# Attention in units of 64 queries: stacked heads in the four quarters of TensorE

## The chip, the cores and the metric

The kernel runs on one core of a Trainium2 chip. The metric is device time in microseconds (us). The core's engines are TensorE (PE, with its weight loads listed as PEld), VectorE (DVE), ScalarE (ACT), GpSimd (POOL) and SyncE (SP), which here issues all DMAs. Each engine runs its own instructions in the order in which the program emitted them; semaphores order the engines among each other.

## What is computed

Causal attention (2 batches, 12 heads, 448 tokens, head width 64, f32) feeds two feed-forward layers. The change lies in the attention alone.

```python
scores = q @ k.T / 8                      # per head, 448 x 448
scores = where(upper triangle, -1e9, scores)
attn = exp(scores - rowmax);  attn /= rowsum + 1e-9
x = attn @ v                              # to (896 tokens, 768)
h = x @ w_in;  x = (h * sigmoid(h)) @ w_out          # 768 -> 2048 -> 768
h = x @ w_in2; solu = h * softmax(h); ln = layernorm(solu) * g; out = ln @ w_out2
```

## The kernel before

Two heads make a pair: their 64-wide q and k lie one above the other in the 128 partitions (head 0 in rows 0 to 63, head 1 in 64 to 127). There are 12 pairs; pairs 0 to 5 are batch 0. `ORDER` is a table of steps written out by hand, in which each step is a letter for the work, the pair, and what part of it; a step emits its instructions at once, so the table sets the order on every engine. The letters:

- `q`, `v`, `w`: a DMA of a pair's q and k, of its v, of a weight chunk.
- `So`, `Sa`, `Sb`, `Sc`: score products on PE into one of four PSUM slots of two banks (`/2` is the slot). For each head, query tiles c = 0, 1, 2 of 128 queries are multiplied with 128, 256 and 384 keys (`scores`, L174). The two heads use the two row halves of the PE array, each with all 128 output columns, and run side by side. The last 64 queries of both heads stand stacked in one tile with 448 keys (`scores_last`, L184). Its two row halves write the same banks, so it is made in two passes, held apart by a relay on SP (`f`, L193).
- `m` (L204, DVE): scale, mask and row maximum of one unit, PSUM to SBUF. `e` (L210, ACT): exp with row sum, in place. `r` (L216, L217, DVE): reciprocals. `n` (L224 on POOL, L222 on ACT, L226 on DVE): multiplication by them; a closing `G`, `A` or `V` names the engine.
- A pair has seven units of 128 rows: three query tiles for each of two heads, 128, 256 and 384 wide, and the stacked one, 448 wide: 2 x (128 + 256 + 384) + 448 = 1984 columns.
- `T` (L238, PE): transposes of a pair's 64 x 128 blocks, in two halves of 16. `x` (L255 on ACT, L253 on DVE): their eviction, in four pieces of 768, 256, 512 and 512 columns.
- `P` (L264, PE): attn times v. The two heads use the two column halves of the array; per head four products of 448, 320, 192 and 64 columns. `h` and `l`: the result split into a rounded part and a rest.
- `ca`, `sh`, `sl`, `rh`, `sp`, `wl`: preparation of the first weight chunks from their 64-bit form (`ca` is L291 on ACT, `wl` is L358 on POOL). `g`: a quarter of the first feed-forward product (L427 to L429, 9 instructions) for two blocks of batch 0, which depend on pairs 0 to 5 alone.

After the table the feed-forward products run on PE; at L427 with output tile h the first of them for batch 1 begins. From there on, weights are prepared by `feed`, one chunk after the other, behind the products. A pair's buffers rotate: four for q and k, four for the exponentials, four PSUM slots.

Of the kernel before, what the change touches and what calls it, by code (L numbers as in the profile page):

```python
# [8 lines left out]
F32 = mybir.dt.float32  # L9
# [9 lines left out]
C = 64  # L19
# [32 lines left out]
UNITS = [(0, 2), (1, 2), (0, 0), (1, 0), (0, 1), (1, 1), (0, 3)]  # L52

# [7 lines left out]
So0/1 Sa0/2 m0.00 m0.10 e0.00 Sb0/0 m0.02 m0.12 e0.02 f0 v5 Sc0 e0.12 v3 e0.10 m0.03 q4 v6 m0.01 Sa1/3 e0.03 m0.11  # L61
e0.01 Sb1/1 m1.10 e0.11 Sb2/2 m1.00 f1 m1.12 v0 Sc1 e1.00 f2 r0 w0 e1.10 m1.02 Sa2/0 n0.10G e1.12 m1.03 n0.12G e1.02
Sc2 m1.11 n0.03G m1.01 e1.03 m2.10 Sa3/3 m2.00 e1.11 m2.12 n0.00G n0.11G e1.01 m2.03 Sb3/1 e2.00 n0.02G m2.02 f3 Sc3
e2.10 m2.11 e2.03 n0.01G r1 Sb4/0 m3.02 e2.11 n1.11G f4 m2.01 q5 e2.12 n1.03G m3.10 v1 T0.0/2 m3.12 e2.02 v7 m3.00
n1.02G m3.11 w1 e2.01 T0.1/3 m3.03 v2 x0.0A Sc4 n1.12G m3.01 v9 r2 x0.1A n1.01G Sa4/1 x0.2V ca0 e3.03 n2.01G x0.3V
T1.1/2 q8 n1.00G e3.10 m4.00 w2 P0/3 m4.10 n2.03G e3.01 m4.01 w3 m4.11 e3.00 m4.03 n2.00G q6 e3.02 n1.10G m4.02
e3.12 n2.11G T1.0/0 m4.12 h0A n2.02G x1.3V Sa5/1 e3.11 n2.12G l0 x1.1A x1.0A x1.2V T2.1/3 n2.10G e4.02 r3 T2.0/0
m5.00 n3.10G e4.11 sh0 P1/2 n3.00G x2.1A x2.3V x2.0A n3.11G m5.12 n3.02G e4.12 x2.2V P2/0 e4.03 m5.10 n3.12G m5.02
h1A sl0 n3.01G e4.10 l1 e4.00 Sb5/3 e4.01 h2V n3.03G T3.0/1 e5.12 f5 q7 r4 T3.1/2 sh1 n4.12G ca3 l2 Sc5 e5.00 x3.2V
x3.0A n4.02G Sa6/0 x3.3V q9 x3.1A n4.11G e5.10 m5.11 Sb6/1 ca1 m6.00 n4.01G m6.12 P3/2 f6 e5.02 v4 n4.03G m5.03  # L70
e5.11 m5.01 e5.03 n4.10G m6.10 m6.02 n4.00G e5.01 T4.1/3 rh0 h3A T4.0/0 sh2 r5 x4.3A Sc6 l3 n5.01G x4.2A sl1 x4.0A
n5.00G Sa7/2 q10 m6.01 x4.1A m6.03 n5.10G e6.12 P4/3 n5.11G m7.00 m6.11 e6.00 n5.12G m7.12 e6.02 m7.02 n5.02G e6.01
m7.10 Sb7/0 h4V e6.10 n5.03G T5.0/1 e7.02 f7 v10 l4 Sc7 e6.11 x5.0V e7.12 T5.1/2 x5.1V e6.03 Sb8/3 rh1 Sa8/1 x5.3A
f8 w4 r6 m7.01 x5.2A n6.02G Sc8 m7.03 e7.00 e7.10 m7.11 n6.01G P5/2 m8.01 e7.01 n6.12G m8.10 sp1 m8.03 e7.11 n6.11G
m8.12 e7.03 m8.02 n6.10G Sa9/0 n6.00G m8.11 h5A n6.03G m8.00 sp0 l5 T6.0/3 e8.01 r7 Sb9/1 e8.12 x6.1V T6.1/2 n7.11G
f9 x6.0V v11 e8.10 Sc9 n7.01G w5 x6.3A m9.02 n7.02G v8 x6.2A P6/3 m9.10 q11 e8.11 m9.11 n7.03G m9.01 n7.00A e8.00
m9.00 n7.12V n7.10G e8.02 m9.03 T7.1/2 wl1 e8.03 m9.12 T7.0/1 x7.2A r8 Sa10/0 x7.3A x7.0V n8.00G n8.10G h6A Sb10/2
n8.01G e9.12 x7.1V m10.00 f10 n8.12G P7/1 l6 e9.10 e9.03 m10.12 n8.11G m10.10 e9.02 n8.02V n8.03G m10.02 e9.00
T8.0/3 h7V e9.01 T8.1/0 wl0 x8.1A l7 e9.11 Sc10 sh3 x8.0A r9 Sa11/1 x8.3V n9.01G n9.02A x8.2V ca2 n9.00G P8/3 n9.11G
n9.10A m10.01 e10.00 m10.03 n9.03G e10.10 e10.12 m11.00 m10.11 n9.12V e11.00 Sb11/0 m11.02 h8A T9.1/2 f11 m11.10  # L80
e10.11 Sc11 m11.12 e10.02 l8 T9.0/1 e10.01 sl2 e10.03 g0 x9.2V e11.02 r10 m11.01 n10.10G e11.12 x9.3V n10.03G x9.1A
g1 m11.11 e11.01 n10.01V n10.00G x9.0A n10.02V n10.11G m11.03 n10.12A e11.11 T10.0/2 rh2 e11.03 sl3 T10.1/1 w6 rh3
e11.10 P9/0 x10.2A x10.0V w7 x10.3A r11 sh4 n11.02A n11.00G n11.12V h9A n11.10G x10.1V P10/1 ca4 n11.01V n11.03A
n11.11V l9 sp2 T11.1/2 sp3 wl2 T11.0/0 ca5 x11.3V g2 x11.0V wl3 x11.2V sh5 x11.1V P11/2 sl4 h10V rh4 l10 g3 w8 h11A
l11
# [4 lines left out]
def fused(ctx, tc, qk, vv, w1, w2, w3, w4, gl, out):  # L90
# [13 lines left out]
    gain = const.tile([128, KF2], F32, name="gain")  # L104

# [16 lines left out]
    with tc.manual_schedule():  # L122
# [4 lines left out]
        mask3 = att.tile([128, S], F32, name="mask3", bufs=1)  # L127
# [4 lines left out]
        QC = 3  # L132
        KEYS = [(0, 0), (0, 1), (0, 2), (1, 0), (1, 1), (1, 2), (0, 3)]
        COL = {u: n for n, u in enumerate(UNITS)}
        AT = {(0, 0): 0, (0, 1): 1, (0, 2): 3, (1, 0): 6, (1, 1): 7, (1, 2): 9, (0, 3): 12}
        wide = lambda c: min(128 * (c + 1), S)

        st = [att.tile([128, 44], F32, name=f"st{n}", tag=f"st{n}", bufs=1) for n in range(4)]
# [37 lines left out]
        def scores_last(p, n, first):  # L176
            k, q = raws[p]
            if first:
                sb[p] = slot(n)
            dst = scs[p, 0, 3] = sb[p][:, :, 256:256 + S // 2]  # L180
            made = []
            for j in range(2):
                r, z = slice(64 * j, 64 * j + 64), j if first else 1 - j
                made.append(nc.tensor.matmul(dst[:, z], q[QC][r], k[r, S // 2 * z:S // 2 * (z + 1)],  # L184
                                             start=first, stop=not first))
            if first:
                passes[p] = made
            else:
                for m in made:
                    behind(m, relays[p])  # L190

        def relay(p):
            relays[p] = nc.sync.nop(nofuse=True)  # L193
            for m in passes[p]:
                behind(relays[p], m)

        def ep(p, u):
            return es[p % EB][:, AT[u]:AT[u] + 4].rearrange("q b k -> q (b k)")[:, :wide(u[1])]

        def maxes(p, u):  # L200
            o, m = ep(p, u), (mask3 if u[1] == 3 else mask)[:, S - wide(u[1]):]
# [975 lines left out]
```

## Time and profile before

| | |
|---|---|
| Runs | 401.73, 400.26, 401.11 us; median 401.11 |
| Profiled execution | 401.01 us; its span, first to last instruction, is 399.2 us |
| Granted TensorE clock, mean over the span | 1.00 |
| PE busy in the span | 98% |
| DVE, ACT, POOL busy | 74%, 70%, 46% |
| DMA | 50.04 MB, mean 125 GB/s |

Busy shares are averages over stages that differ. The attention takes roughly the first fifth of the span, and matmuls are pipelined with modelled ends, so PE's share alone does not say how near it is to its limit. Instructions on ACT and DVE overlap too: the distance between two starts is what one of them costs its engine.

### The profile page before, as it was taken

The page shows a single profiled execution, that of the slowest core. Times are in us where ns is not written, and L with a number is a line of the kernel's source. Part 1 is how long each engine was busy: PE and PEld are TensorE (multiplying, and loading weights), DVE is VectorE, ACT ScalarE, POOL GpSimd, SP SyncE. Part 2 cuts the span into 40 slices and gives each one's busy share as a digit, 9 for nine tenths or more (in the row PEclk, how much of TensorE's full clock was granted, in tenths as well). Part 3 has the DMA queues.
Part 4 walks back from the last instruction along what each step waited for, and adds up shares of the span by engine and source line. Part 5 has one row for each costly group of instructions (what it writes and reads, how often), then busy time and mean ns, then how long its engine had stood idle before and what let it go on. Part 6 is the DMA issues. An engine that isn't in the chain of part 4 may idle for free.

```text
span 399.2 us, 7580 instructions
## 1 busy us (share of the span) xinstructions
PE 392.2 (98%) x2622; PEld 363.1 (91%) x2622; DVE 295.9 (74%) x693; ACT 281.1 (70%) x653; POOL 183.9 (46%) x219
## 2 busy tenths in 40 slices
PE   7999999999999999999999999999999999999996
PEld 5777678899999999999999999999988888999996
DVE  4999999677675765768566667776899997666943
ACT  5999999655665473766577777785757875898630
POOL 2998783223554372556665445554001000496450
PEclk9999999999999999999999999999999999999999
DMA  7775322134434333437344567777023320011121
GB/s 246 248 276 173 121 91 65 56 92 151 150 98 125 112 113 112 120 120 201 115 150 129 164 178 233 244 252 217 18 81 98 101 79 0 2 61 39 42 79 61
DMA packets 19766, 50.04 MB, mean 125 GB/s; under 512 B 2320, under 2 KB 4496, under 8 KB 19728
## 3 DMA queue, kind: packets, MB, share of 16 engines
q1 hardware_dynamic: 19728, 49.56, 39.4%
q8 instruction: 21, 0.34, 0.4%
q14 instruction: 17, 0.14, 0.1%
HBM read 46.80 MB, written 2.75 MB: 124 GB/s over the span
## 4 chain that ended last, share of the span: by engine, by line
PE 89%; DVE 8%; ACT 2%; issue 1%; DVEq 0%; ACTq 0%; SPq 0%
PE h L427 8%; PE h L429 8%; PE h L428 8%; PE x L264 5%; PE ps L942 5%; PE h L598 4%; PE h L597 4%; PE h L599 4%; PE ps L944 4%; PE ps L943 4%; PE h L865 3%; PE h L867 3%; PE h L866 3%; PE x L174 3%; PE x L238 3%; DVE e L204 3%
## 5 line engine op out<-in xcount | busy, mean ns | idle before, releaser
L291 ACT ACTIVATE wr<-wr 128x384 f32<-128x384 f32 x96 | 56.9, 592 | 9.4 <-DMA wr<-w_in 9.4
L428 PE MATMUL h<-l,wh 128*128 128x448 f32 x174 | 61.3, 352 | 0.0
L427 PE MATMUL h<-h,wh 128*128 128x448 f32 x174 | 61.3, 352 | 0.0
L429 PE MATMUL h<-h,wl 128*128 128x448 f32 x174 | 61.3, 352 | 0.0
L224 POOL TENSOR_TENSOR e<-e,st 128x128 f32<-128x128 f32 (+3 forms) x70 | 44.0, 666 | 20.1 <-DVE st L217 15.1
L321 DVE SCALAR_TENSOR_TENSOR pw<-wr,pw 128x384 uint32<-128x384 uint32 x77 | 43.0, 559 | 12.9 <-ACT pw L317 12.7
L446 POOL TENSOR_TENSOR gl<-sg,gh 128x448 fp32r<-128x448 f32 x29 | 32.8, 1152 | 38.9 <-ACT sg L444 38.9
L210 ACT ACTIVATE e<-e,st 128x128 f32<-128x128 f32 (+3 forms) x84 | 43.8, 536 | 4.2 <-DVE st L204 4.2
L358 DVE TENSOR_TENSOR wl<-pw,wh 128x384 fp32r<-128x384 f32 x29 | 16.2, 557 | 31.7 <-ACT wh L354 31.7
L354 ACT ACTIVATE wh<-pw 128x384 fp32r<-128x384 f32 x29 | 14.3, 494 | 35.2 <-PE h L428 27.4
L204 DVE CUSTOM_DVE_ANT_0 e<-x,mask 128x128 f32<-128x128 f32 (+3 forms) x84 | 32.9, 445 | 5.2 <-PE x L174 5.1
L428 PEld LDWEIGHTS h<-l,wh 128*128 128x128 f32 x174 | 32.9, 189 | 0.1
L427 PEld LDWEIGHTS h<-h,wh 128*128 128x128 f32 x174 | 32.9, 189 | 0.0
L429 PEld LDWEIGHTS h<-h,wl 128*128 128x128 f32 x174 | 32.9, 189 | 0.0
L896 POOL TENSOR_TENSOR s<-s,mhalf 128x1 f32<-128x1 f32 x7 | 4.2, 596 | 62.3 <-DVE s L895 62.3
L865 PE MATMUL h<-w3h,h 128*128 128x512 f32 x84 | 32.0, 381 | 0.6 <-ACT h L893 0.6
L866 PE MATMUL h<-w3l,h 128*128 128x512 f32 x84 | 31.9, 379 | 0.0
L867 PE MATMUL h<-w3h,l 128*128 128x512 f32 x84 | 31.8, 379 | 0.0
L597 PE MATMUL h<-gh,wh 128*128 128x448 f32 x90 | 31.7, 352 | 0.0
L599 PE MATMUL h<-gh,wl 128*128 128x448 f32 x90 | 31.7, 352 | 0.0
L598 PE MATMUL h<-gl,wh 128*128 128x448 f32 x90 | 31.7, 352 | 0.0
L358 POOL TENSOR_TENSOR wl<-wx,wh 128x384 fp32r<-128x384 f32 x21 | 21.2, 1011 | 22.7 <-ACT wh L354 22.7
(299 smaller groups left out, 1115.1 us busy)
## 6 DMA issues: line engine op xcount, KB each, us to landing
wr<-w_in SPq DMA_DIRECT2D x96, 384.0 KB, 3.2
qk<-qk_in SPq DMA_DIRECT2D x11, 480.0 KB, 4.6
v<-vv_in SPq DMA_DIRECT2D x12, 256.0 KB, 5.2
out<-o SPq DMA_DIRECT2D x14, 192.0 KB, 1.9
qk<-qk_in SPq DMA_DIRECT2D x2, 128.0 KB, 2.3
qk<-qk_in SPq DMA_DIRECT2D x1, 224.0 KB, 2.6
gain<-gl_in SPq DMA_DIRECT2D x1, 4.0 KB, 3.8
```

The costliest lines, as they stand in the source:

```text
L204: nc.vector.tensor_tensor_reduce(o, scs[p, u[0], u[1]], m, -SCALE, 3.0e38, ALU.add, ALU.min, st[p % 4][:, COL[u]:COL[u] + 1])
L210: nc.scalar.activation(ep(p, u), ep(p, u), AF.Exp, bias=st[p % 4][:, n:n + 1], scale=-1.0, accum_out=st[p % 4][:, 8 + n:9 + n])
L224: eng.tensor_tensor(ep(p, u), ep(p, u), r.to_broadcast([128, wide(u[1])]), ALU.mult)
L291: nc.scalar.activation(high, high, AF.Copy, scale=DOWN)
L427: nc.tensor.matmul(ps[:, :S], wh, rh, start=turn == 0 and k % NB == 0, stop=False)
L428: nc.tensor.matmul(ps[:, :S], wh, rl, start=False, stop=False)
L429: nc.tensor.matmul(ps[:, :S], wl, rh, start=False, stop=turn == 1 and k % NB == NB - 1)
L597: nc.tensor.matmul(ps[:, :S], wh, rh, start=f == CF[0], stop=False)
L598: nc.tensor.matmul(ps[:, :S], wh, rl, start=False, stop=False)
L599: nc.tensor.matmul(ps[:, :S], wl, rh, start=False, stop=f == CF[-1])
L865: nc.tensor.matmul(ps[:, n], yh[k][:, at], wh, start=k == 0, stop=False)
L866: nc.tensor.matmul(ps[:, n], yh[k][:, at], wl, start=False, stop=False)
```

## The change

The unit of attention becomes 64 queries of both heads of a pair, stacked: unit u holds queries 64u to 64u + 63 of head 0 and head 1 in its two row halves, and has 64(u + 1) keys. A pair has seven units, 64 to 448 wide: 1792 columns. Every score product now has 64 rows of weights and 64 output columns, a quarter of the PE array. In units 1 to 4 (`SWAPPED`) head 0 goes to the lower half of the output partitions and head 1 to the upper; so a unit in 0, 5, 6 uses the two quarters on one diagonal of the array and a unit in 1 to 4 the two on the other. The lists `STEPS_A` and `STEPS_B` cut the products so that, from pair 1 on, groups of four equally long ones in the four quarters follow each other (320, 128, 64 columns; 256 and 128). Both products of a unit write one PSUM bank, in different partitions. Pair 0 has an order of its own (`Sx`, `Sy`, `Sz`) that follows its three DMA pieces.

Transposes stay 32 per pair, their evictions become 896, 128, 640 and 384 columns. `P` has the same columns, but cut at the units where the head order turns (`RUNS`): eight products per head in place of four. The relay and the second mask go. A pair's q and k are 448 KB, before 480. In the table, five weight conversions (`ca`) go from ACT to POOL, a sixth goes behind the table, and one weight chunk less is prepared in it (`EARLY` was fed one further). The letters for engines are dealt anew: normalizations 74 on POOL, 3 on ACT, 7 on DVE (before 70, 6, 8); evictions 26 on ACT and 22 on DVE (before 24 and 24); `h` 9 on ACT and 3 on DVE (before 8 and 4).

```diff
-UNITS = [(0, 2), (1, 2), (0, 0), (1, 0), (0, 1), (1, 1), (0, 3)]
+UNITS = S // C
+SWAPPED = (1, 2, 3, 4)
+BANKS = ((6, 0), (4, 2), (5,), (3, 1))
+RUNS = ((0, 1, 0), (1, 5, 1), (5, 7, 0))
 ORDER = """
-So0/1 Sa0/2 m0.00 m0.10 e0.00 Sb0/0 m0.02 m0.12 e0.02 f0 v5 Sc0 e0.12 v3 e0.10 m0.03 q4 v6 m0.01 Sa1/3 e0.03 m0.11
+q1 v0 q2 v1 Sx0/0 q3 m0.1 Sy0 m0.0 v2 e0.1 e0.0 Sz0 m0.2 m0.3 e0.2 m0.4 e0.3 m0.5 e0.4 q4 m0.6 Sa1/2 e0.5 w0 v3 e0.6
...
-        def scores(p, c):
-            k, q = raws[p]
-            for j in range(2):
-                r = slice(64 * j, 64 * j + 64)
-                t = sb[p][:, 1 - j] if c == 1 else sa[p][:, j, 384:] if c == 0 else sa[p][:, j]
-                scs[p, j, c] = dst = t[:, :wide(c)]
-                nc.tensor.matmul(dst, q[c][r], k[r, :wide(c)], start=True, stop=True)
...
+        def scores(p, steps):
+            a = raws[p]
+            for u, lo, hi in steps:
+                n = next(n for n, bank in enumerate(BANKS) if u in bank)
+                t = (sa, sb)[n // 2][p][:, n % 2]
+                o = sum(wide(v) for v in BANKS[n][:BANKS[n].index(u)])
+                scs[p, u] = t = t[:, o:o + wide(u)]
+                for j in range(2):
+                    r, z = slice(64 * j, 64 * j + 64), 64 * (j ^ (u in SWAPPED))
+                    nc.tensor.matmul(t[z:z + 64, lo:hi], a[r, 0, C * u:C * u + C], a[r, 1, lo:hi], start=True, stop=True)
...
+        STEPS_A = [(6, 0, 320), (4, 0, 320), (6, 320, 448), (2, 0, 128), (0, 0, 64), (2, 128, 192)]
+        STEPS_B = [(5, 0, 256), (3, 0, 256), (5, 256, 384), (1, 0, 128)]
...
+        PARTS_T = [[(0, range(UNITS)), (3, range(6, UNITS))], [(1, range(2, UNITS)), (2, range(4, UNITS))]]
+        HALVES = [[(u, kb) for kb, us in part for u in us] for part in PARTS_T]
...
             for z in range(NKB):
-                for j in range(2):
-                    nc.tensor.matmul(t[64 * j:64 * j + 64, 128 * z:S], v[:, j, z], aT[p][:, z, j, 128 * z:],
-                                     start=z == 0, stop=z == NKB - 1)
+                for lo, hi, swap in RUNS:
+                    sl = slice(C * max(lo, 2 * z), C * hi)
+                    for h in range(2):
+                        j = h ^ swap
+                        if sl.start < sl.stop:
+                            nc.tensor.matmul(t[64 * j:64 * j + 64, sl], v[:, j, z], aT[p][:, z, h, sl],
+                                             start=z == lo == 0, stop=z == NKB - 1, skip_group_check=True)
...
-        def conv_a(n, c):
+        def conv_a(n, c, eng=None):
             r = wraw[n, c]
             high = r[:, :, 1].bitcast(F32)
-            nc.scalar.activation(high, high, AF.Copy, scale=DOWN)
+            if eng is nc.gpsimd:
+                eng.tensor_tensor(high, high, down.to_broadcast([128, CH]), ALU.mult)
+            else:
+                nc.scalar.activation(high, high, AF.Copy, scale=DOWN)
...
-        fed[0] = EARLY + 1
-        pend.append(EARLY)
+        fed[0] = EARLY
```

On PE, around the middle of the attention, the order before reads as follows (L184 and L174 are score products, L238 transposes, L264 attn times v; the columns after the tile names are outputs x moving columns, and the count).

```order
L264 MATMUL x_586<-aT,v_168 64x64 x2
L238 MATMUL x_609<-ident,e_97 128x64 x16
L238 MATMUL x_628<-ident,e_97 128x64 x16
L184 MATMUL x_579<-qk 128x224 x2
L174 MATMUL x_579<-qk 128x256 x2
L174 MATMUL x_661<-qk 128x384 x2
L174 MATMUL x_661<-qk 128x128 x2
L264 MATMUL x_673<-aT,v_597 64x448 x2
L264 MATMUL x_673<-aT,v_597 64x320 x2
L264 MATMUL x_673<-aT,v_597 64x192 x2
L264 MATMUL x_673<-aT,v_597 64x64 x2
```

Transposes and scores follow each other there without a change of form. The same round of the changed kernel (L160 are score products, L204 transposes, L231 attn times v):

```order
L231 MATMUL x_354<-aT,v_146 64x64 x2
L204 MATMUL x_390<-ident,e_98 128x64 x16
L204 MATMUL x_411<-ident,e_98 128x64 x16
L160 MATMUL x_432<-qk 64x320 x4
L160 MATMUL x_432<-qk 64x128 x4
L160 MATMUL x_432<-qk 64x64 x4
L160 MATMUL x_450<-qk 64x256 x4
L160 MATMUL x_450<-qk 64x128 x4
L231 MATMUL x_463<-aT,v_150 64x64 x2
L231 MATMUL x_463<-aT,v_150 64x256 x2
L231 MATMUL x_463<-aT,v_150 64x128 x2
L231 MATMUL x_463<-aT,v_150 64x192 x2
```

Before, scores and transposes share one tile form, 64 rows by 128 columns, and PE changes form twice a round; now scores are 64 by 64, and it changes three times. From the first warm-up product to the first product of batch 1 the whole order has 24 changes of form before and 37 now.

On POOL, pairs 2 and 3 before (L224 are normalizations, e_99 and e_100 the exponentials of the two pairs):

```order
L224 TENSOR_TENSOR e_99<-e_99,st_103 128x256
L224 TENSOR_TENSOR e_99<-e_99,st_103 128x384 x2
L224 TENSOR_TENSOR e_99<-e_99,st_103 128x128
L224 TENSOR_TENSOR e_100<-e_100,st_104 128x128 x2
L224 TENSOR_TENSOR e_100<-e_100,st_104 128x256
```

There POOL does nothing but normalizations. Now (L190 are normalizations, L259 the weight conversion that stood on ACT):

```order
L190 TENSOR_TENSOR e_99<-e_99,st_103 128x384
L190 TENSOR_TENSOR e_99<-e_99,st_103 128x256
L259 TENSOR_TENSOR wr<-wr,down 128x384
L190 TENSOR_TENSOR e_100<-e_100,st_104 128x128
L190 TENSOR_TENSOR e_100<-e_100,st_104 128x192
L190 TENSOR_TENSOR e_100<-e_100,st_104 128x384
```

The conversion now stands in POOL's queue ahead of pair 3's normalizations; three more stand ahead of those of pairs 4 and 5, the fifth ahead of pair 9's.

## Rows read from the trace of the kernel before

**Rows 1.** Page, part 1: busy us, share of the span, instructions
```profile
PE 392.2 (98%) x2622; PEld 363.1 (91%) x2622; DVE 295.9 (74%) x693; ACT 281.1 (70%) x653; POOL 183.9 (46%) x219
```

**Rows 2.** Stretches: us, busy PE, PEld, DVE, ACT, POOL, then PEclk, DMA share, GB/s
```profile
10.00:20.00 10.00, 9.38 (x118) 7.49 (x116) 9.62 (x49) 10.00 (x38) 9.16 (x15) 1.00 0.72 246
...
60.00:70.00 10.00, 10.00 (x118) 7.99 (x118) 9.62 (x30) 9.77 (x31) 3.26 (x6) 1.00 0.24 70
...
80.00:100.00 20.00, 20.00 (x107) 19.98 (x106) 14.93 (x30) 11.43 (x27) 5.75 (x6) 1.00 0.41 123
```

**Rows 3.** Chain, first 80 us: start us, us, engine, tile, line
```profile
3.62 2.01 PE x L174 x8
...
16.65 0.71 PE x L238 x16
...
19.11 0.49 PE x L238 x16
...
21.49 0.65 PE x L238 x16
...
29.77 0.43 PE x L184 x4
30.21 1.30 PE x L174 x12
...
31.89 1.88 PE x L264 x16
...
59.79 0.58 PE x L184 x4
...
70.69 1.24 PE x L238 x32
...
77.84 0.19 PE h L427
```

**Rows 4.** Timeline of PE, a moment of L264
```profile
31.82 0.60 PE L264 MATMUL x<-aT,v 128*64 128x448 f32 x2
```

**Rows 5.** Timeline of ACT from 20.2 us: start us, us, instruction
```profile
20.21 0.40 ACT L210 ACTIVATE e<-e,st 128x128 f32<-128x128 f32 x1
...
20.59 0.62 ACT L210 ACTIVATE e<-e,st 128x384 f32<-128x384 f32 x1
...
21.19 0.61 ACT L210 ACTIVATE e<-e,st 128x384 f32<-128x384 f32 x1
```

**Rows 6.** Timeline of ACT, a weight conversion and what follows it
```profile
31.44 0.58 ACT L291 ACTIVATE wr<-wr 128x384 f32<-128x384 f32 x1
31.88 0.63 ACT L210 ACTIVATE e<-e,st 128x384 f32<-128x384 f32 x1
```

**Rows 7.** Timeline of DVE from 20.0 us
```profile
20.03 0.42 DVE L204 CUSTOM_DVE_ANT_0 e<-x,mask 128x256 f32<-128x256 f32 x1
...
20.38 0.62 DVE L204 CUSTOM_DVE_ANT_0 e<-x,mask 128x448 f32<-128x448 f32 x1
...
20.92 0.55 DVE L204 CUSTOM_DVE_ANT_0 e<-x,mask 128x384 f32<-128x384 f32 x1
```

**Rows 8.** Timeline of POOL: three pairs' normalizations, in brackets the idle before
```profile
29.39 4.37 POOL L224 TENSOR_TENSOR e<-e,st 128x384 f32<-128x384 f32 x7 [0.36 <-PE x L238]
35.13 4.69 POOL L224 TENSOR_TENSOR e<-e,st 128x256 f32<-128x256 f32 x7 [1.38 <-DVE st L217]
42.12 4.37 POOL L224 TENSOR_TENSOR e<-e,st 128x384 f32<-128x384 f32 x7 [2.30 <-DVE st L217]
```

**Rows 9.** Groups by line and form, first 76 us: xcount, busy us, mean ns
```profile
L224 POOL TENSOR_TENSOR e<-e,st 128x384 f32<-128x384 f32 x16 | 13.0, 828 | 2.7 <-DVE st L217 2.3 <-PE x L238 0.4
...
L358 POOL TENSOR_TENSOR wl<-wx,wh 128x384 fp32r<-128x384 f32 x4 | 4.0, 1008 | 1.6 <-ACT wh L354 1.6
```

More of the change, by code (lines that the diff above doesn't have):

```diff
@@ L64 @@
[L64 to L78, printed above, removed]
@@ L130, in fused, with load_pair @@
         es = [att.tile([128, 16, 128], F32, name=f"e{n}", tag=f"e{n}", bufs=1) for n in range(EB)]
[L132 to L138, printed above, removed]
+        AT = [sum(v // 2 + 1 for v in range(u)) for u in range(UNITS)]
+        wide = lambda u: C * (u + 1)
+        st = [att.tile([128, 24], F32, name=f"st{n}", tag=f"st{n}", bufs=1) for n in range(4)]
         raws, vs = {}, {}
-        QW = (QC + 1) * 128
-        QUERIES = {0: 0, 2: 128 + S, 1: 256 + S, QC: 384 + S}
-        def load_pair(p, pieces=((0, QW + S),)):
+        def load_pair(p, pieces=((0, S),)):
             b, hp = divmod(p, NP)
-            a = att.tile([128, QW + S], F32, name="qk", tag=f"qk{p % QB}", bufs=1)
+            a = att.tile([128, 2, S], F32, name="qk", tag=f"qk{p % QB}", bufs=1)
             for lo, hi in pieces:
-                nc.sync.dma_start(a[:, lo:hi], qk[b, hp, :, lo:hi])
-            raws[p] = (a[:, 128:128 + S], {c: a[:, o:o + 128] for c, o in QUERIES.items()})
+                nc.sync.dma_start(a[:, :, lo:hi], qk[b, hp, :, :, lo:hi])
+            raws[p] = a
         def load_v(p):
@@ L176, in scores_last @@
[L176 to L181, printed above, removed]
-            for j in range(2):
[L183 to L195, printed above, removed]
+        sa, sb = {}, {}
+        def scores(p, steps):
[8 more added lines that the diff above has]
+                    nc.tensor.matmul(t[z:z + 64, lo:hi], a[r, 0, C * u:C * u + C], a[r, 1, lo:hi], start=True, stop=True)
@@ L197, in ep, with steps @@
+        def steps(*us):
+            return [(u, 0, wide(u)) for u in us]
+        STEPS_A = [(6, 0, 320), (4, 0, 320), (6, 320, 448), (2, 0, 128), (0, 0, 64), (2, 128, 192)]
+        STEPS_B = [(5, 0, 256), (3, 0, 256), (5, 256, 384), (1, 0, 128)]
         def ep(p, u):
[L198 removed]
+            return es[p % EB][:, AT[u]:AT[u] + u // 2 + 1].rearrange("q b k -> q (b k)")[:, :wide(u)]
         def maxes(p, u):
[L201 removed]
@@ L505, in g1drain, with scores_to, first_scores @@
             gemm1(f, half, 0, turn)
-        def scores_a(p, n):
-            sa[p] = slot(n)
-            for c in (2, 0) if p else (2,):
-                scores(p, c)
-        def scores_ahead(p, n):
-            sa[p] = slot(n)
-            scores(p, 0)
+        def scores_to(tiles, p, n, us):
+            if n is not None:
+                tiles[p] = slot(n)
+            scores(p, us)
+        def first_scores(p, n):
+            sb[p] = slot(1)
+            scores_to(sa, p, n, steps(0, 1))
         emit = {
-            "So": lambda p, n, u, e: scores_ahead(p, n), "Sa": lambda p, n, u, e: scores_a(p, n), "Sb": lambda p, n, u, e: scores_last(p, n, True),
-            "Sc": lambda p, n, u, e: (scores_last(p, n, False), scores(p, 1)), "f": lambda p, n, u, e: relay(p),
+            "Sx": lambda p, n, u, e: first_scores(p, n), "Sy": lambda p, n, u, e: scores(p, steps(2, 3)),
+            "Sz": lambda p, n, u, e: scores(p, steps(5, 4, 6)),
+            "Sa": lambda p, n, u, e: scores_to(sa, p, n, STEPS_A), "Sb": lambda p, n, u, e: scores_to(sb, p, n, STEPS_B),
             "q": lambda p, n, u, e: load_pair(p), "v": lambda p, n, u, e: load_v(p),
@@ L1141, in heads_T @@
         return a.transpose(0, 1, 3, 2).reshape(B, NP, 128, S)
-    cut = 128 * (NKB - 1)
     q, k = heads_T(inputs["q"]), heads_T(inputs["k"])
-    last = np.zeros((B, NP, 2, D, 2, C), np.float32)
-    for j in range(2):
-        last[:, :, j, :, j] = q[:, :, D * j:D * j + D, cut:]
     v = np.zeros((B, NP, 2, 128 * NKB, D), np.float32)
```

95 lines of the change are left out of this document (43 added, 52 removed).

## The prediction

> **What bounds the kernel now.** I read the page's busy shares first [rows 1]: PE at 98%, PEld at 91%, so PE looks like the bound everywhere. The table of stretches corrects this for the attention [rows 2]: from 10 to 20 us ACT is busy 10.00 us of 10, DVE 9.62, PE 9.38 and POOL 9.16, and from 60 to 70 us PE, ACT and DVE are still within 0.4 us of full. From 80 us PE is busy 20.00 of 20 and DVE, ACT and POOL have slack. So the attention has three engines at their limit at once, and what follows has one, PE. The chain of waits shows where the attention ends [rows 3]: the first transposes at 16.65 us, the last pair's at 70.69, the first product of batch 1 (output h, L427) at 77.84. Whatever moves that last start moves the end by the same amount, as long as the products behind it, which the change leaves alone, stay fed.
>
> **What the 77.84 us consist of on PE.** A pair's scores cost 0.43 + 1.30 + 0.43 us (two L184 passes, of which a row shows one, and the three L174 tiles) [rows 3]: 2.16 us for 2 x 224 + 256 + 384 + 128 = 1216 columns, two products side by side, 1.78 ns a column. attn times v costs 1.88 us, the transposes about 1.1 (0.49 us for 16 without a change of form before them, 0.65 with one). A product quarter of nine takes 9 x 0.19 = 1.7, and there are four. Sum: 12 x (2.16 + 1.88 + 1.1) + 6.9 = 68.6 us. Of these, some 8.6 (the scores of four pairs) lie before the first transposes at 16.65, so 60.0 us of work fill 61.2 us of time. PE, too, is full; a saving on one engine alone would buy little.
>
> **The change, part by part.**
>
> Scores on PE. From pair 1 on the groups have 320 + 128 + 64 + 256 + 128 = 896 columns. If four products run side by side as two do now, that is 896 x 1.78 = 1.59 us, 0.57 less per pair, 6.3 us over 11 pairs. The trace shows the two halves of this apart: L184 and L174 pair up on row halves, and L264 on column halves (two 448-wide products open together within one 0.60 us row) [rows 3, 4]; it never shows both at once. I take four abreast, since each splitting by itself runs without loss. Bounds: 0.57 gained, or, at two abreast, 1792 x 1.78 = 3.19 us, 1.03 lost.
> The Trainium skill ("TensorEngine Tiling (Array Packing)", Tiling Modes) says that tiles operate independently and load weights and multiply in parallel; by that rule the gain is the one just taken. The Trainium skill ("TensorEngine Tiling (Array Packing)", Restrictions and Gotchas) also says that different row tiles cannot access the same PSUM bank at the same time; a unit's two products come from two row halves and write one bank, so by that rule they would run one after the other and the loss is the one just named. No row shows two row halves writing one bank together: before, they had two banks, or the relay between them.
>
> Pair 0. Units 2 and 3 use the same two quarters and unit 6 stands alone, so its columns are 128 + 192 + 256 + 384 + 448 = 1408 against 1216. At 1.78 ns that is 0.3 us more, at the opening's rate (512 columns in 2.01 us, 3.9 ns each [rows 3]) 0.75; I take 0.5.
>
> Changes of form. The order has 37 on PE where it had 24. The rows price one: 16 transposes take 0.49 us behind scores, 0.65 behind attn times v; a score pass takes 0.43 behind transposes, 0.58 behind attn times v [rows 3]. 13 x 0.155 = 2.0 us more.
>
> attn times v. The same columns, eight more products a pair. Its 16 instructions run at 1.84 ns a column, and 64-column transposes start every 0.49 / 16 = 31 ns without loss. I take 0. If each extra product cost a start of that kind, 8 x 31 ns x 12 = 3.0 us would be added; that is the other end.
>
> PE in sum: -6.3 + 0.5 + 2.0 = -3.8 us.
>
> ACT. One exp of 128 columns costs 0.38 us from start to start, one of 384 0.60 [rows 5]: 0.86 ns a column plus 0.27. Seven per pair as before, 1984 - 1792 = 192 columns fewer: 0.165 us a pair, 2.0 in all. Six conversions leave it at 31.88 - 31.44 = 0.44 us each [rows 6]: 2.6. Three normalizations fewer and smaller ones (704 columns for 1856): 1.3. Two more evictions with 1024 more columns: +0.9 to +1.0; one more h of 448 columns: +0.4. Sum -4.6 us.
>
> DVE. Maxima of 256 and 448 columns cost 0.35 and 0.54 us [rows 7]: 0.99 ns a column, 192 fewer in each of 12 pairs, -2.3 us; evictions, 1024 columns and two starts fewer, -1.1. The fewer h, the smaller normalizations and the chunk prepared later come on top. At least -3.4.
>
> POOL. Five conversions more. POOL does not do this one in the trace; the nearest rows of 384 columns are 0.83 us (one tensor and a broadcast column, which is its form) and 1.01 (two tensors) [rows 9]. Bounds 4.1 to 5.1, and 4 more normalizations with 64 more columns, under 1 us. The cover: before a pair's normalizations POOL stood idle 0.36, 1.38 and 2.30 us [rows 8]; its seven now have 192 columns fewer. So I count 0, and the loss of that cover is a rival below.
>
> The chunk left for later. The table ends with four chunks, the fifth half as far as before. PE has 36 products of 0.19 us, 6.8 us, before it needs it, and between 80 and 100 us DVE was idle 5.1 us and ACT 8.6 [rows 2]; I count 0, and at most two conversion steps, some 2 us, if it is late. DMA moves 32 KB less a pair and is not late from 10 us on: 0.
>
> **The sum.** Three engines get shorter by 3.8 (PE), 4.6 (ACT) and at least 3.4 us (DVE, with more on top). They wait for one another in turn, so the stage shortens by about the least of them; with DVE's uncounted pieces that is PE: 3.8. From 401.0, the profiled execution's own time (399.2 of span and 1.8 around it; the median of the runs is 401.1), this gives 397.2 us. Its own range, with the three engines not fitting perfectly or PE's early start of transposes helping, is 395 to 399.
>
> **The rivals.**
>
> 1. *More is won: about 394.* Pair 0's seven units are the first in POOL's queue, so its transposes may start some 3 us before 16.65. For: PE's early idle time is recovered then, on top of 3.8. Against: ACT is full from 10 us on and cannot give more than its 4.6 plus a little in the opening.
>
> 2. *POOL takes the gain: about 401.* Four conversions stand ahead of pairs 3, 4 and 5 (twice). A pair's seven normalizations take 4.4 us by [rows 8], now 4.0; with a conversion 4.9, about the 54.0 / 11 = 4.9 us at which pairs now follow each other on PE [rows 3]. If each pushes the transposes behind it by 0.8 to 1.0 us, 3.2 to 4.0 us go and the time stays where it is. For: no slack in that count. Against: the idle time in [rows 8], and that the shift carries only to pairs that PE already waits for.
>
> 3. *Slower: two abreast, about 413.* The four quarters do not run side by side, since a unit's halves exclude each other in their bank. Scores then cost 3.19 us: 12 x 1.03 + 2.0 for the changes of form = 14.4 us on PE, less the 1.2 us in which it waited and about 1 us of the earlier start: some 12 us over 401.0. It decides from the point at which a pair's scores fall short of 2.16 - 2.5 / 11 = 1.93 us, that is at 1086 columns of 1.78 ns: a fifth of the overlap lost is enough to turn the sign. For: nothing in the trace shows four. Against: each of the two splittings runs without loss.
>
> **How the numbers follow.** Chances: the forecast 0.50, rival 1 0.15, rival 2 0.13, rival 3 0.17, and 0.05 for part of rival 3 (three abreast, or attn times v paying its 3.0 us), 402 to 406. A difference within 0.5%, 2 us, is what a measurement of this kernel cannot tell from none. The forecast and rival 1 are faster (0.65), rival 2 the same (0.13), the rest slower (0.22). The range from 393 to 403 holds the forecast, rival 2, most of rival 1 and a little of the partial case, 0.8 together; rival 3 is left out.
>
> **What would show it.** In the changed profile a pair's five score groups should take about 1.6 us on PE, with four products open at a time; 3 us there is rival 3. Transposes behind scores should now take 0.65 for 16. ACT's distance between exps of one width should be as before, and POOL should show the conversions at 0.8 to 1.0 us, with idle time left before the pairs' normalizations; if PE's transposes wait for POOL between pairs 3 and 6 it is rival 2. The first product of batch 1 should start near 74 us, and PE should be busy 20.00 of 20 us behind it. The prediction is wrong if that start comes later than 76 us, or if PE then waits for the fifth weight chunk.

## The result: 0.56% slower, and the profile after

402.74 us median of ten runs (402.13 to 404.74) against 400.68 of before (400.17 to 401.73); ratio 1.0056, 95% interval 1.0038 to 1.0074. The forecast was 397.2. The profiled execution took 404.74 us, 402.5 of them its span: it is the slowest of the ten, 2.0 us above their median, and the three whose clock stayed at 1.000 took 402.13 to 402.35, so its rows show more loss than most runs had.

The page's busy shares, to be read against [rows 1]:
```profile
PE 390.8 (97%) x3042; PEld 366.4 (91%) x3042; DVE 295.2 (73%) x689; ACT 278.3 (69%) x648; POOL 189.6 (47%) x235
```
PE and ACT are busy for less time, as forecast, and the kernel takes longer. The stretches of [rows 2], and behind them the first half of the attention cut finer:
```profile
10.00:20.00 10.00, 5.84 (x100) 4.65 (x104) 7.67 (x39) 9.55 (x36) 7.50 (x13) 0.75 0.97 366
60.00:70.00 10.00, 9.77 (x177) 8.18 (x173) 9.78 (x30) 8.81 (x31) 8.57 (x13) 1.00 0.14 41
80.00:100.00 20.00, 20.00 (x108) 19.98 (x107) 14.31 (x30) 13.68 (x29) 6.74 (x6) 1.00 0.38 120
...
12.00:16.00 4.00, 0.28 (x2) 0.14 (x2) 4.00 (x22) 4.00 (x17) 3.65 (x6) 0.87 1.01 376
16.00:20.00 4.00, 3.81 (x58) 3.11 (x62) 2.15 (x9) 3.56 (x14) 3.85 (x8) 0.50 0.89 346
20.00:24.00 4.00, 4.00 (x68) 2.98 (x62) 3.79 (x18) 2.27 (x10) 1.78 (x4) 0.78 0.42 139
```
The loss is in the first row: PE worked 5.84 us there, where it had 9.38 before. From 12 to 16 us it did next to nothing (0.28) while DVE and ACT were full, and from 16 to 20 us the granted clock is 0.50, the lower of its two levels, where before it was 1.00 throughout. DVE and ACT then wait in their turn (2.15 of 4 us; 2.27 of 4).

The chain of waits, to be read against [rows 3]; columns as there:
```profile
12.37 3.78 POOL e L190 x6
16.14 0.05 issue
16.19 1.86 PE x L204 x22
18.05 3.19 PE x L160 x40
21.24 2.18 PE x L231 x32
23.42 1.14 PE x L204 x32
24.56 1.73 PE x L160 x40
...
45.11 1.68 PE x L160 x40
46.80 1.91 PE x L231 x32
...
81.19 0.19 PE h L397
```
Pair 0's transposes (L204), but for two of the 32, wait for six normalizations on POOL and start at 16.19, nearly where they did (16.65). The scores of pair 3 (L160) take 3.19 us at half clock; one row further on, at full clock, the same 40 records take 1.73, later 1.68: four abreast, against 2.16 of before. The first product of batch 1 starts at 81.19 instead of 77.84, 3.35 us late, and behind it nothing changed: 402.5 - 81.19 = 321.3 us, before 399.2 - 77.84 = 321.4.

What PE did until then, worked out from its records (each moment counted once; this count ends some 0.16 us ahead of the chain's row). Pairs 0 to 4 had been scored when before's first attn times v began, pairs 0 to 3 in the changed kernel:

| us of PE | before | after | experiment: three slow pairs |
|---|---|---|---|
| start to first attn times v | 19.54 | 21.17 | 18.50 |
| of it idle / scores | 2.74 / 12.71 | 5.96 / 10.84 | 3.00 / 11.92 |
| from there: scores | 16.05 (7 pairs) | 13.99 (8 pairs) | 14.00 (8 pairs) |
| attn times v | 22.41 | 23.57 | 23.31 |
| transposes | 12.04 | 13.12 | 13.38 |
| products of batch 0 | 7.47 | 7.44 | 7.44 |
| idle | 0.18 | 1.73 | 2.01 |

Before, the chain has its first attn times v here (in the changed kernel at 21.24, above):
```profile
19.61 1.88 PE x L264 x16
```
In this execution the opening costs 1.63 us, and behind it -2.06 + 1.16 + 1.08 - 0.03 + 1.55 = 1.70 come on top. The last column is a run whose clock stayed at 1.00: its opening is 1.04 us shorter than before's, and behind it stand -2.05 + 0.90 + 1.34 - 0.03 + 1.83 = 1.99. Of the changed kernel's idle 1.73 us there, 0.7 end with a rest `l` on DVE, 0.4 with an eviction on ACT, 0.2 with a maximum on DVE.

POOL, against [rows 8] and [rows 9]: pairs' normalizations with conversions (L259) between them, then the conversions' group:
```profile
31.37 0.83 POOL L259 TENSOR_TENSOR wr<-wr,down 128x384 f32<-128x384 f32 x1
33.28 4.04 POOL L190 TENSOR_TENSOR e<-e,st 128x192 f32<-128x192 f32 x7 [1.08 <-ACT e L177]
37.28 1.94 POOL L259 TENSOR_TENSOR wr<-wr,down 128x384 f32<-128x384 f32 x2
...
44.12 4.04 POOL L190 TENSOR_TENSOR e<-e,st 128x320 f32<-128x320 f32 x7 [0.43 <-ACT e L177]
...
L259 POOL TENSOR_TENSOR wr<-wr,down 128x384 f32<-128x384 f32 x5 | 4.4, 896 | 0.0
```
There is still idle time ahead of the groups (1.08, 0.43), so POOL isn't the bound in the middle.

The theories taken into the experiments: A, PE's wait lets the clock fall, and that is paid in full; B, pair 0 comes late, by waits of its own and by full DVE and ACT; formed after the first four runs, C, POOL's greater load; and, after the first eight, D: what the first pairs' faster scores save is idle time at once. Each kernel was timed in five rounds beside before; "first product" below is that of batch 1, from the profiled execution.

### The profile page after: what moved, and what is told of

The parts are those of the page before. It is cut to its first block, busy times and chain, and to the rows that moved or that the text cites. A ratio compares the mean times of both kernels' runs of the same rounds, so it can differ in the third digit from the quotient of the medians.

```text
span 402.5 us, 8420 instructions
## 1 busy us (share of the span) xinstructions
PE 390.8 (97%) x3042; PEld 366.4 (91%) x3042; DVE 295.2 (73%) x689; ACT 278.3 (69%) x648; POOL 189.6 (47%) x235
## 4 chain that ended last, share of the span: by engine, by line
PE 82%; DVE 10%; ACT 4%; POOL 2%; DMA 1%; issue 1%; SPq 0%; DVEq 0%; ACTq 0%
PE h L397 8%; PE h L399 8%; PE h L398 8%; PE ps L906 4%; PE h L562 4%; PE h L561 4%; PE h L563 4%; PE ps L908 4%; PE ps L907 4%; PE x L160 4%; PE h L829 3%; PE h L831 3%; PE h L830 3%; ACT e L177 3%; PE x L231 2%; DVE w3l L328 2%
## 5 line engine op out<-in xcount | busy, mean ns | idle before, releaser
L261 ACT ACTIVATE wr<-wr 128x384 f32<-128x384 f32 x91 | 53.8, 592 | 8.3 <-DMA wr<-w_in 8.1
L190 POOL TENSOR_TENSOR e<-e,st 128x128 f32<-128x128 f32 (+6 forms) x74 | 44.6, 635 | 19.1 <-DVE st L172 10.9
L177 ACT ACTIVATE e<-e,st 128x320 f32<-128x320 f32 (+6 forms) x84 | 41.7, 500 | 8.9 <-DVE st L172 8.7
L328 DVE TENSOR_TENSOR wl<-pw,wh 128x384 fp32r<-128x384 f32 x30 | 16.7, 557 | 32.9 <-ACT wh L324 32.9
L172 DVE CUSTOM_DVE_ANT_0 e<-x,mask 128x128 f32<-128x128 f32 (+6 forms) x84 | 31.1, 415 | 9.2 <-PE x L160 8.8
L328 POOL TENSOR_TENSOR wl<-wx,wh 128x384 fp32r<-128x384 f32 x21 | 21.9, 1044 | 21.4 <-ACT wh L324 21.3
```

The costliest lines, as they stand in the source:

```text
L261: nc.scalar.activation(high, high, AF.Copy, scale=DOWN)
L328: eng.tensor_tensor(l, wx.pop((n, c)), h.bitcast(F32), ALU.subtract)
```

## The experiments

**20 unread products** (on PE ahead of the first transposes).
```diff
-... n0.0G v5 T0.1/3 r1 ...
+... n0.0G v5 y20 T0.1/3 r1 ...
+def idle_products(count):
+    for _ in range(count):
+        nc.tensor.matmul(sb[1][:, 0, :S], xl[0][:, :128], xl[0][:, :S], start=True, stop=True)
```


> Added: 20 products of 128 x 448 whose result nobody reads, on TensorE between the scores of pair 2 and the first transposes; nothing else moves. In the changed kernel TensorE is idle there from 12.0 to 16.2 us but for two transposes, and the granted clock then reads 0.50 until 21.8 us. Theory A (that idle time brings the clock down, and the half clock is paid in full because TensorE sets the pace behind it): granted clock 1.00 through 10 to 22 us, the transposes of pair 0 in 1.3 us instead of 1.9, pair 3's scores in 1.7 instead of 3.2, first product of batch 1 near 78.0 us instead of 81.2, time 399.0 to 400.5 us. Theory B (what pair 0 loses is lost on VectorE and ScalarE, which are busy then, and the clock is hidden behind them): the clock reads 1.00 but the first product of batch 1 stays above 80.5 us, time 402 to 403 us.


Measured: 404.44 us, ratio 1.0077 (1.0064 to 1.0090); mean clock 0.999 or 1.000 in all six runs. Its stretches:
```profile
12.00:16.00 4.00, 2.48 (x23) 2.20 (x16) 4.00 (x22) 4.00 (x18) 3.70 (x6) 1.00 1.00 395
16.00:20.00 4.00, 3.85 (x55) 3.09 (x57) 1.87 (x9) 2.17 (x9) 3.85 (x8) 1.00 0.84 326
```
and its chain:
```profile
18.20 1.21 PE x L204 x32
19.41 1.68 PE x L160 x40
21.09 1.91 PE x L231 x32
```
The clock stays up, and transposes and scores take 1.21 and 1.68 us instead of 1.86 and 3.19. But the 20 products had to wait for VectorE's maxes (their tile is read until 13.7 us) and put the transposes back from 16.19 to 18.20. The first product comes at 81.18, where it was. So keeping the clock is worth the 2.0 us that were lost in front of it; the run doesn't decide A against B by itself.

**10 unread products.** The same with `y10`.


> As the experiment with 20 unread products before the first transposes, but with 10, so that they end near 15.9 us, when the transposes can begin anyway (the 20 waited for VectorE until 13.7 us and ran until 18.0, which put the transposes back by 2 us, while the full clock behind them gave 2 us back). Theory A (each microsecond of half clock behind the transposes is half a microsecond of TensorE's time, paid in full): clock 1.00 in every run, span near 400.0 us in every run, as in those runs of the changed kernel whose clock did not fall; time 402.0 to 402.4 us, and none at 403.5 or more. Theory B (what is lost is lost on VectorE and ScalarE, the clock is beside the point): times spread from 402 to 404.7 us as in the changed kernel.


Measured: 402.72 us, ratio 1.0050 (1.0030 to 1.0069), runs from 401.90 to 404.46. A's expectation failed: in the profiled run the clock fell all the same (0.64 from 16 to 20 us, mean 0.994) and its time was 404.46; and one run at mean clock 1.000 took 403.74, one at 0.999 took 403.12, so the clock is not all of the spread. What bears A out is the changed kernel's own ten runs: three at mean clock 1.000 took 402.13, 402.21 and 402.35, three at 0.996 took 402.27, 402.34 and 403.13, four at 0.991 or 0.992 took 403.67 to 404.74. The fall costs about 2 us where it is long, 0 to 0.9 us where it is short, and the kernel without it is still some 1.5 us slower than before.

**Pair 0 in three score tiles** (maxes of units 2 and 3 no longer wait for units 4 to 6).
```diff
-... m0.1 Sy0 m0.0 v2 e0.1 e0.0 Sz0 m0.2 m0.3 e0.2 ...
+... m0.1 m0.0 Sy0 v2 e0.1 e0.0 m0.2 m0.3 Sz0 e0.2 ...
+low, mid, top = slot(0), slot(1), slot(3)
```


> Pair 0's scores alone are put into three score tiles instead of two, so that the maxes of units 2 and 3 no longer wait for the products of units 4 to 6, and are written in front of those products. Theory B (the opening's waits are carried to the end): the exponentials of pair 0 end near 10.6 us instead of 11.7, the transposes of pair 0 begin near 15.1 instead of 16.2, the first product of batch 1 comes 1 us earlier, time near 401.7 us. Theory A (the fall of the clock is what counts, and it still falls here since TensorE still waits 4 us for GpSimd's seven normalisations): transposes 1 us earlier at half clock, the clock back 1 us earlier too, so the same 1 us at the most; a granted clock that doesn't fall would be against A. No gain at all (402.7 us) if ScalarE only waits later instead.


Measured: 402.51 us, ratio 1.0041 (1.0028 to 1.0053); the intervals of this and of the changed kernel overlap. Pair 0's exponentials end at 10.4 us as expected, but the transposes start at 15.9, only 0.3 us earlier, because its reciprocals stand on DVE behind pair 1's maxes. First product 80.00; the clock still fell (0.67 from 16 to 20 us).

**Pair 0's normalizations on three engines.**
```diff
-... n0.1G m1.3 w1 n0.4G ... n0.2G Sb2/1 e1.6 m1.0 n0.5G Sa2/0 ... n0.6G ... n0.3G ...
+... n0.2G m1.3 w1 n0.6A n0.3G ... n0.5V Sb2/1 n0.4G e1.6 m1.0 n0.1G Sa2/0 ...
```


> Of pair 0's seven normalisations one of 448 goes from GpSimd to ScalarE and one of 384 to VectorE, and GpSimd takes those that the first transposes need first. Theory A (TensorE's wait for GpSimd and the half clock that follows): the first transposes begin near 14 us instead of 16.2 and run on, the idle stretch is 2 us instead of 4, the clock stays at 1.00 or falls for a shorter time; first product of batch 1 at 77 to 79 us, time 398 to 400.5 us. Rival (ScalarE and VectorE are full there, so what GpSimd gives off comes back as later exponentials and maxes of pair 2): transposes of pair 0 earlier, those of pair 1 not, time 402 to 403.5 us.


Measured: 403.51 us (402.33 to 404.54), ratio 1.0056 (1.0038 to 1.0074). In the profiled run (402.33 us):
```profile
13.08 1.75 PE x L204 x32
...
16.24 3.12 PE x L160 x40
19.36 1.91 PE x L231 x32
```
The transposes come 3 us earlier (0.8 of it because pair 0's exponentials ended that much earlier in this run), and then PE waits for pair 3's score tiles until 16.24: the wait has moved from POOL to DVE's maxes of pair 2, and the clock falls there (0.61). No gain that can be measured: ahead of 20 us PE waits for the softmax engines, now for one and now for another.

**Two abreast** (no unit's heads swapped).
```diff
-SWAPPED = (1, 2, 3, 4)
+SWAPPED = ()
-RUNS = ((0, 1, 0), (1, 5, 1), (5, 7, 0))
+RUNS = ((0, 1, 0), (1, 5, 0), (5, 7, 0))
```


> One half of the change undone: no unit's heads are swapped, so all score products of a pair lie on the same two quarters of the array and only two stand side by side; tiles, order and counts stay. If four abreast is worth what was worked out (1.7 us a pair now, 2.9 to 3.2 us by the two-abreast rows), eleven pairs cost 13 to 16 us more, less at most 4 us of idle time that TensorE has in the opening: time 412 to 418 us. Rival (products on other quarters don't run side by side beyond two, the 1.7 us come from the smaller tiles): time 402 to 404 us.


Measured: 413.87 us, ratio 1.0318 (1.0305 to 1.0332). Its chain:
```profile
15.54 1.15 PE x L204 x30
16.69 3.19 PE x L160 x40
19.88 1.91 PE x L231 x32
...
22.93 3.22 PE x L160 x40
```
3.22 us a pair where four abreast takes 1.73, at the same clock. Two things are to be read here. Behind the first attn times v its eight pairs' scores take 25.83 us, 11.8 more than the changed kernel's 13.99, and the time is 11.1 us more: there a pair's scores are paid nearly in full. Ahead of it four pairs are also slower, and yet attn times v starts at 19.88, before the changed kernel's 21.24, whose clock had fallen. Against the next run, at the same clock, the fourth of these pairs is paid too: its scores stand behind the transposes, take 3.19 us for 1.68, and attn times v starts at 19.88 for 18.57. The first three cost nothing: the transposes start at 15.54 for 15.74.

**Three slow pairs.** Units are swapped only from pair 3 on.
```diff
+SLOW = 3
-r, z = slice(64 * j, 64 * j + 64), 64 * (j ^ (u in SWAPPED))
+r, z = slice(64 * j, 64 * j + 64), 64 * (j ^ (u in SWAPPED and p >= SLOW))
-j = h ^ swap
+j = h ^ (swap and p >= SLOW)
```


> The changed kernel with the scores of pairs 0 to 2 back on two quarters (no swapped units there) and four abreast only from pair 3 on. By the forecast's own sum, in which every pair's cheaper scores are a gain, three slower pairs cost 3 x 1.5 us: time near 407 us. Theory D (what the first three pairs' scores save is idle time at once, since the first transposes wait for GpSimd's normalisations, and the idle time then brings the clock down): scores of pairs 0 to 2 end near 13.9 us instead of 12.0, the transposes still run near 16 us, but at full clock, pair 3's scores behind them in 1.7 us instead of 3.2; the granted clock is 1.00 in every run, and the time is 400.5 to 402.5 us: no slower, or faster, with slower scores.


Measured: 402.69 us (402.42 to 402.96, all at 0.998 or more), ratio 1.0042 (1.0029 to 1.0055). Its chain:
```profile
11.91 3.78 POOL e L191 x6
15.74 1.15 PE x L205 x30
16.89 1.68 PE x L161 x40
18.57 1.91 PE x L232 x32
...
78.79 0.19 PE h L398
```
This is the run that decides. Worked out from the records, the three pairs keep PE busy for 10.37 us instead of 7.79, 2.6 us more (not the 4.5 expected: pair 0 takes as long either way), and the median stays: the scores end at 14.1 us instead of 12.0, POOL's normalizations end at 15.69 (16.15 in the changed kernel; pair 0's exponentials end 0.45 us earlier in this run), and the clock stays up. D holds: of the gain of a faster score, that of the first three pairs is worth next to nothing, and in the changed kernel it becomes an idle stretch that can bring the clock down. (Against the changed kernel's runs at full clock, 402.13 to 402.35, the slow scores cost 0.3 to 0.6 us, not 2.6.)

**Conversions back on ScalarE.**
```diff
-... ca0G ... ca1G ... ca2G ... ca3G ... ca4G
+... ca0 ... ca1 ... ca2 ... ca3 ... ca4
```


> One part of the change undone: the five conversions of weight chunks go back from GpSimd to ScalarE (about 0.4 us each on ScalarE before, 0.9 us each on GpSimd now). Theory C (GpSimd's load slows VectorE and makes the normalisations late in the second half): GpSimd 4.4 us less, steps of pairs 4 to 9 earlier, time 0.5 to 1.5 us lower, 401.3 to 402.3 us. Theories A and B (the loss is in the first 24 us, before any conversion): within 0.5 us of the changed kernel, 402.2 to 403.2 us.


Measured: 404.94 us, ratio 1.0095 (1.0079 to 1.0110), first product 81.51. Theory C has the wrong sign: the conversions on POOL are a gain. How large isn't clear, since the clock fell in each of these five runs: at mean clock 0.992 they took 404.68 to 405.21, the changed kernel at 0.991 and 0.992 403.67 to 404.74, so of the 2.2 us between the medians about 0.9 is left at the same clock.

**One unread product in pair 0's first gap.** `Sx0/0 W1 q3` for `Sx0/0 q3`.


> The changed kernel with one unread product between pair 0's first and second scores, where TensorE waits 0.4 us for the second piece of queries and keys, and nothing else. In the changed kernel a 320-wide product took 737 ns until 8 us and 430 ns behind. If that gap keeps TensorE slow, the fast products begin 1 to 2 us earlier, pair 0's exponentials end near 10.5 us instead of 11.7. Theory D: the time gains little by it (0 to 0.7 us), since the first transposes wait for seven normalisations on GpSimd anyhow, only as much earlier as these begin, and the clock still falls behind in some runs. By the sum of TensorE's time alone: 1 to 2 us.


Measured: 403.63 us (402.42 to 404.59), ratio 1.0060 (1.0043 to 1.0078). Pair 0's exponentials end at 10.2 us instead of 11.7 and the transposes start at 14.7, but the clock falls behind them (0.61 from 16 to 20 us) and the time gains nothing that can be measured.

**The opening pulled together** (three score tiles and three engines, as above, in one), then with unread products, then with five more steps moved.
```diff
-Sx0/0 q3 m0.1 Sy0 m0.0 ... Sz0 m0.2 m0.3 ... m1.4 Sb1/3 m1.2 e1.4 r0 ...
+Sx0/0 q3 m0.1 m0.0 Sy0 ... m0.2 m0.3 Sz0 ... r0 m1.4 Sb1/3 m1.2 e1.4 ...
+scores(p, [(4, 0, 320), (6, 0, 320), (6, 320, 448), (5, 0, 384)])
```


> The opening pulled together: pair 0's scores in three score tiles with units 4 and 6 side by side, its reciprocals in front of pair 1's maxes, its normalisations shared by three engines. If the opening is what eats the gain (scores of pair 0 at 12 us and then nothing for TensorE until 16.2), the first transposes begin at 12.5 to 13.5 us, pair 3's scores near 15, and the first product of batch 1 2 to 4 us earlier: time 398.5 to 401 us. Rival (VectorE and ScalarE are full from 9 us on and pace what follows, whatever TensorE could begin): transposes earlier, pair 3's scores still at 16 us or later, time 401.5 to 403.5 us.

> The pulled opening with one unread product more between pair 0's first and second scores and three before the first transposes, against the slow product rate at the start (a 320-wide product took 737 ns before 8 us in the changed kernel and 430 behind) and against the fall of the clock. Theory A: the clock stays at 1.00, time 0.5 to 1.5 us below that of the pulled opening alone. If the clock is beside the point: equal, or 0.2 to 0.6 us slower by the products' own length.

> The pulled opening with its unread products, and five steps moved where TensorE waited: the evictions of pair 0's transposes ahead of pair 2's exponentials on ScalarE (TensorE waited 0.8 us for them), pair 1's and pair 7's low parts ahead on VectorE (0.6 and 0.4 us), one eviction of pair 4 ahead on ScalarE (0.4 us), the last pair's last eviction on ScalarE (0.4 us). If TensorE sets the pace, as its idle time of 2.3 us behind 20 us says, nearly all of it comes back: first product of batch 1 at 75.5 to 76.5 us instead of 77.8, time 399 to 400.2 us. Rival (ScalarE and VectorE are as full as TensorE and hand each wait on): 401 us or more.


Measured: 402.15 us, ratio 1.0026 (1.0011 to 1.0041); with the products 401.36, ratio 1.0011 (1.0001 to 1.0021), all eleven runs at 0.999 or more; with the moved steps 401.77, ratio 1.0014 (1.0005 to 1.0022). The second is the best version found: by the ratios it wins back 1.8 us of the 2.1. Its first attn times v starts at 18.1 us, 1.4 ahead of before's, and its first product at 77.99, 0.2 us behind before's: what the opening wins is lost behind it, and it does not beat before. The third shows that these moves brought no more: the waits taken away came back further on (its attn times v of pair 0 starts another 1.0 us earlier, its first product at 78.25). That DVE and ACT are as full as PE is the likely reason (from 16 to 20 us ACT is busy 4.00 us of 4, DVE 3.85, PE 3.69); it was not shown apart.

## Why the prediction was wrong

*Four abreast: right.* Forecast 1.59 us a pair, measured 1.68 to 1.73; rival 3 is out. Its price was near (413 forecast, 413.87 with two abreast), in part by luck: it charged twelve pairs 1.03 us, 12.4 in all, where that run's scores behind the first attn times v take 25.83 - 16.05 = 9.8 us more than before's. The Trainium skill's rule that "Different row tiles cannot access same PSUM bank simultaneously" ("TensorEngine Tiling (Array Packing)", Restrictions and Gotchas), by which rival 3 was built, does not hold here: a unit's two products come from two row halves, write one bank, and the pair still takes 1.73 us and not 3.22.

*Changes of form and attn times v: near in sum, in part by luck.* Forecast 2.0 + 0, for 13 more changes; the orders as run have 39 where before had 24, 15 more (37 and 13 were a miscount), 2.3 us at the same price. Behind the first attn times v the two kinds cost 1.16 (attn times v) and 1.08 (transposes) more. But 0.5 of the 1.08 are 16 transposes that stood ahead of it before (352 records for 336), and an undisturbed attn times v takes 1.91 us for 1.88, 0.4 us over twelve pairs; the rest of the 1.16 is half clock and waits.

*ACT, DVE, POOL: the gain of the first two was over-estimated.* The stretch from the start to the first product, before and then after (columns as in [rows 2]):
```profile
0.00:77.84 77.84, 74.93 (x858) 55.64 (x859) 69.07 (x257) 68.70 (x218) 50.78 (x93) 1.00 0.48 162
```
```profile
0.00:81.19 81.19, 73.50 (x1278) 58.98 (x1279) 67.93 (x252) 65.58 (x214) 56.47 (x109) 0.96 0.43 148
```
ACT is 3.1 us shorter (forecast 4.6; 1.1 us of the next stage now fall into the stretch), DVE 1.1 (at least 3.4), POOL 5.7 longer (4.1 to 5.1, and under 1 for normalizations). POOL's conversions took 0.90 us each, between the bounds, and rival 2 is out by the idle time in front of the groups and by the experiment that took them off. DVE's missing 2.3 us are slower operations, of the kind that the last section shows: two steps of the weights' preparation took 850 and 520 ns on average instead of 552 and 345, five times each, 2.4 us in all (before, then after; columns as in [rows 9]).
```profile
L303 DVE SCALAR_TENSOR_TENSOR wx<-wr,wx 128x384 uint32<-128x384 uint32 x5 | 2.8, 552 | 0.0
L308 DVE TENSOR_SCALAR wr<-wr 128x384 uint32<-128x384 uint32 x6 | 2.1, 345 | 0.0
```
```profile
L273 DVE SCALAR_TENSOR_TENSOR wx<-wr,wx 128x384 uint32<-128x384 uint32 x5 | 4.3, 850 | 0.0
L278 DVE TENSOR_SCALAR wr<-wr 128x384 uint32<-128x384 uint32 x5 | 2.5, 520 | 0.0
```
By the prediction's own rule of the least of the three, DVE's 1.1 us alone would have left little gain; whether DVE's time counted as such, no run shows.

*Pair 0: mis-sized.* Forecast 0.5 us; its exponentials end at 11.7 us where before's ended at 10.1. A 320-wide product took 737 ns until 8 us and 430 ns behind, and a 0.4 us wait for the second piece of queries and keys came on top. The views read a granted clock of 1.00 all through the opening, but the trace's first row of it stands at 8.13 us, before's at 6.60, and in both the products are slow until just then (before: 844 ns for 384 columns, then 482). Part of that is the run's and not the change's: in the profiled runs of five kernels with this same beginning the first row stands anywhere from 5.43 to 8.64 us.

*The sum: this failed.* "They wait for one another in turn, so the stage shortens by about the least of them", and that least was PE's 3.8. The 3.8 held 6.3 us "over 11 pairs", as if a pair's scores were worth the same wherever they stand. The prediction even had the number that contradicts it: some 8.6 us of scores lie before the first transposes, and those start when the softmax of pair 0 lets them, at 16.65 us before and 16.19 after. Three pairs made 2.6 us slower there cost 0.3 to 0.6 us. Scores ahead of that point are cover for a wait. Before used it to score five pairs until the first attn times v; the changed kernel scored four, faster, and then stood idle (5.96 us for 2.74). So behind the first attn times v the gain counts for seven pairs only, 16.05 - 7 x 1.75 = 3.8 us (that this equals the forecast's 3.8 is chance), and one more pair's scores, 1.75, stand there. That leaves 16.05 - 13.99 = 2.06 us, and the 2.2 us of the two other kinds eat it. What remains in the profiled run is 1.63 us of a later start and 1.55 us of PE's idle time behind it. The later start comes with the fallen clock: in the run with three slow pairs, at full clock, the start is earlier than before's, and there the other kinds (2.24 us) and PE's idle time (1.83) alone outweigh the faster scores (2.05) and the earlier start (1.04).

*Rival 1 did not come.* It took the transposes to start some 3 us earlier, since pair 0's units stand first in POOL's queue; they start 0.46 us earlier. The experiment that did start them 3 us earlier (13.08 us) found the next wait directly behind, on DVE.

*What wasn't thought of:* that an idle stretch of a 98% busy engine has a price of its own. PE was idle from 12.0 to 16.2 us but for two transposes, and the clock stood at 0.50 for what followed, about 2 us in the runs that have it long.

Open: the time around the span is 1.8 us before (401.01 for 399.2) and 2.2 after (404.74 for 402.5), 0.4 us of the 2.06 between the medians (402.74 - 400.68). It goes with what POOL is given: 1.8 in all five runs with the conversions back on ScalarE, 2.0 where two of pair 0's normalizations left POOL, 2.2 in all the others; why, no view shows. Open too are the two slow runs at full clock with 10 unread products, and what a profile of the changed kernel at full clock would show, since none was taken. That a fifth pair of scores ahead of the first attn times v, as before has it, would help was not tried in the changed kernel: its score tiles are all taken there.

## What to carry to other kernels

Before a saving is multiplied by its count, find the first point at which the engine is what others wait for, and count only the instances behind it; ahead of it, faster work turns into idle time. Where an engine runs ahead of a wait, count how many units it gets done until then as a stock: a change that keeps the wait and shrinks the stock can lose, although each unit became faster. To test whether a speed-up counts at a place, make it slow again at that place alone.

## What the runs showed of the hardware

The granted clock of TensorE fell to 0.50 at 14.95 us in the changed kernel's profile, PE having done only two transposes since 12.0 us, and rose to 1.00 at 21.78. In the kernel with 10 unread products PE did nothing from 12.2 to 14.0 us only, and the clock fell in the profiled run too, at 15.47; with 20 of them, after a gap from 12.2 to 13.7 us, it stayed at 1.00. It also differed between runs of one kernel (mean 0.991 to 1.000).

Two of VectorE's operations from and to SBUF took 1.8 and 2.4 times as long while POOL was at work. The timeline of DVE in the changed kernel, the same operation (L273, L266) twice:
```profile
70.21 0.55 DVE L266 SCALAR_TENSOR_TENSOR wx<-wr 128x384 uint32<-128x384 uint32 x1
...
71.52 0.51 DVE L273 SCALAR_TENSOR_TENSOR wx<-wr,wx 128x384 uint32<-128x384 uint32 x1
...
73.48 1.00 DVE L266 SCALAR_TENSOR_TENSOR wx<-wr 128x384 uint32<-128x384 uint32 x1
74.52 1.24 DVE L273 SCALAR_TENSOR_TENSOR wx<-wr,wx 128x384 uint32<-128x384 uint32 x1
```
and POOL's at the same time:
```profile
71.77 2.29 POOL L190 TENSOR_TENSOR e<-e,st 128x128 f32<-128x128 f32 x3 [2.67 <-DVE st L183]
74.03 1.32 POOL L328 TENSOR_TENSOR wl<-wx,wh 128x384 fp32r<-128x384 f32 x1
```
0.55 and 0.51 us with POOL idle through the first and the first half of the second, 1.00 and 1.24 beside it, and POOL's own L328 takes 1.32 where [rows 9] have 1.01. The Trainium skill ("GPSIMD Engine Reference", Specifications) lists the SBUF interfaces as shared with VectorE; the trace agrees. What it cost here isn't shown: PE was busy for 9.88 of the 10 us from 70 to 80, but the chain of waits to the last attn times v passes through both slow operations.
